# Linear attention with a gated feed-forward block: w2 loaded on the ScalarE queue, layer norms ahead of key finals, two tiny reads at the head

## The chip, the cores and the metric

One core of a Trainium2 chip runs the whole program. The metric is the device time of one execution in microseconds (us), median of several executions. A profile is one more execution, traced; its times are counted from the first instruction and its span is a little shorter than the device time (239.8 against 241.5 us for the profiled run of the kernel before). Engine names in the profile: PE is TensorE's matmuls, PEld its weight loads, DVE is VectorE, ACT is ScalarE, POOL is GpSimd, SP is SyncE; "SPq" and "ACTq" are the two that issue DMAs here.

## The reference, cut to what matters

The input x has 2048 tokens of 640 features, in bf16. The kernel normalizes it, and computes a linear attention and a relu feed-forward of the same normalized x:

```
xn  = layernorm(x)
q,k,v = split(xn @ wqkv)                  # 32 heads of 20
pq, pk = phi(q), phi(k)                   # phi(t) = (t+1 if t>0 else exp(t)) + 1e-6
kv  = sum over tokens of pk * v ;  z = sum over tokens of pk
s   = (pq @ kv) / (pq . z + 1e-6) @ wo
g   = silu(relu(xn @ w1) @ w2)            # w1: 640x1728, w2: 1728x640
out = x + s * g
```

## The kernel before

The program is written per engine: each operation is put on one engine's list in program order, with the waits that its reads and writes need. An engine takes its list strictly in order. So the order of the lines below is the order on each engine, and an operation that waits holds all that come behind it on the same engine (the load of w2 is held so until 134.8 us, as shown below).

The 2048 tokens are 16 tiles of 128, or four chunks j = 0 to 3 of 512. Chunk 0 is only centred at first (its scale is applied when its products are evicted), transposed on TensorE, and feeds the keys of tiles 0 to 3 and the w1 products `H_block(0, f)`. Tiles 4 to 15, and later tiles 0 to 3 for their queries, are normalized on VectorE and transposed by DMA. The helpers that matter:

```
def aggr(t):                    # VectorE: mean and variance; GpSimd: (var + eps) ** -0.5
    sc.op("DVE", bn_aggr -> mv[t]); sc.op("POOL", add -> rsv[t]); sc.op("POOL", pow -> rsy[t])
def LN_norm(t):                 # VectorE: (x - mean) * rsy, bf16 128x640; then x for tile t+8 is loaded
    last_norm[0] = sc.op("DVE", ... xn[:, t, :] ...)
    if t + XR < T: x_load(t + XR)
def xnT_dma(t):                 # SyncE queue: DMA transpose of xn[t] into xnT
def K_mm(t, b) / K_exp / K_relu # key product of a tile; two ScalarE evictions (exp, relu)
def K_fin(t):                   # VectorE: min(exp, 1) + 1e-6, then add relu -> pk[t]
    zpend.append(t)
def z_add():                    # GpSimd: zacc += pk[t]   (f32 128x640)
    t = zpend.pop(0)
    sc.op("POOL", ... tensor_tensor(out=zacc, in0=zacc, in1=pk[:, t, :], op=ALU.add))
def Q_block(j, f):              # five matmuls; ScalarE exp; two VectorE instructions -> pqT
```

The main loop walks the w1 blocks ("h") and query blocks ("q") of each chunk as TensorE's work, and hangs everything else on item numbers n:

```
kat  = [{5: 4, 7: 5, 9: 6, 11: 7}, {7: 8, 11: 9, 15: 10, 19: 11}, {6: 12, 9: 13, 12: 14, 15: 15}, {}]
lnat = [{0: 4, 2: 5, 4: 6, 6: 7}, {0: 8, 4: 9, 8: 10, 12: 11}, {0: 12, 3: 13, 6: 14, 9: 15}, {}]
for j in range(J):
    for n, item in enumerate(plans[j]):
        ... Q_block or H_block ...
        if n in lnat[j]:
            t = lnat[j][n]
            LN_stats(t)
            if j == 0:
                K_fin(t - 4)
                LN_norm(t);     xnT_dma(t)
                LN_norm(t - 4); xnT_dma(t - 4)
        ...                                   # j > 0: LN_norm and xnT_dma one item later
        if n in kat[j]: K_mm, K_exp, K_relu, K_fin of tile kat[j][n]
        if n >= 3 and zpend and len(zpend) > (1 if j < J - 1 else 0):
            z_add()
        ...                                   # chunk 3: z_split at n=2, z_col at 8, den() at 14
```

`den()` computes the denominator's reciprocal, writes it 20-fold to DRAM (`scr`, four writes of 640 KB) and reads it back (five reads). After the loop, on SyncE's queue, in this order: the `scr` writes and reads of `den()`, w2 (which waits for the last w1 product, as it takes w1's place), wo. Then TensorE computes `G_block(0..4)` (160 matmuls of keys against xn) and the w2 products `U_sub`, which fill the rest of the program.

## Time and profile before

Time before: 240.54 us median of 3 runs (240.16 to 243.49). From the first two parts of the page: the span is 239.8 us, and TensorE is busy for most of it.

```profile
...
PE 219.2 (91%) x1425; PEld 134.0 (56%) x1436; DVE 112.5 (47%) x211; ACT 87.8 (37%) x144; POOL 45.0 (19%) x69
...
PEclk9999999999999999999999995799999999999998
...
```

The first line is each engine's busy time, share of the span and number of instructions. The second cuts the span into 40 slices of 6 us: the clock granted to TensorE, in tenths. It drops to half in slices 24 and 25 (counted from 0); the trace has half clock from 142.8 to 153.0 us. As TensorE is 91% busy, what can be won is mostly its idle time. The list of waits of TensorE (engine, line, what it waited for; us in total, times, longest) says where that is:

```profile
PE psT L811 <- DMA reg<-in_B_w_dram: 9.5, 1, 9.5
PE psT L471 <- DMA reg<-reg: 2.9, 3, 2.3
PE psT L471 <- DMA reg<-in_A_wqkv_dram: 1.7, 1, 1.7
...
PE psT L471 <- ACT hT L550: 0.7, 1, 0.7
...
```

The first is the w2 product waiting for w2; the second is key products of tiles 4 to 15 waiting for a DMA transpose (2.3 us at 32.8 us is the longest); the third is the first key product waiting for its weights. The chain of waits (start, duration, what) shows why w2 is late:

```profile
...
114.74 3.36 DVE regE L660
...
121.77 10.71 DMA scr<-regE
...
134.30 0.47 SPq L672
...
135.31 13.15 DMA reg<-in_B_w_dram
...
148.55 3.62 PE psT L811 x13
...
```

The reciprocal (L660) ends at 118.1, the fourth write of `scr` lands at 132.5, the five reads behind it are issued until 134.8, only then is w2 issued, and it lands at 148.5. TensorE had finished G at 139.04. The clock was cut during that long idle stretch, 3.75 us after it began, and stayed so until 153.0: the first 13 w2 matmuls took 3.62 us, later sets in this chain mostly 1.77.

### The profile page before, as it was taken

The page shows a single profiled execution, that of the slowest core. Times are in us where ns is not written, and L with a number is a line of the kernel's source. Part 1 is how long each engine was busy: PE and PEld are TensorE (multiplying, and loading weights), DVE is VectorE, ACT ScalarE, POOL GpSimd, SP SyncE. Part 2 cuts the span into 40 slices and gives each one's busy share as a digit, 9 for nine tenths or more (in the row PEclk, how much of TensorE's full clock was granted, in tenths as well). Part 3 has the DMA queues.
Part 4 walks back from the last instruction along what each step waited for, and adds up shares of the span by engine and source line. Part 5 has one row for each costly group of instructions (what it writes and reads, how often), then busy time and mean ns, then how long its engine had stood idle before and what let it go on. Part 6 is the DMA issues. An engine that isn't in the chain of part 4 may idle for free.

```text
span 239.8 us, 3474 instructions
## 1 busy us (share of the span) xinstructions
PE 219.2 (91%) x1425; PEld 134.0 (56%) x1436; DVE 112.5 (47%) x211; ACT 87.8 (37%) x144; POOL 45.0 (19%) x69
## 2 busy tenths in 40 slices
PE   6899969999999989999999912999999999999994
PEld 5554434555545544444577701767776776777672
DVE  3388995999847981560600000482132432224143
ACT  5496635566655655554212130023202110210211
POOL 2154673333241365200000050000000000000000
PEclk9999999999999999999999995799999999999998
DMA  6998740511101120000099799920010101000011
GB/s 190 353 296 178 165 113 12 164 29 27 31 0 27 30 52 3 0 0 3 15 211 211 262 386 338 363 79 0 3 55 27 57 27 55 30 27 29 28 55 56
DMA packets 26992, 23.90 MB, mean 100 GB/s; under 512 B 11744, under 2 KB 26336, under 8 KB 26976
## 3 DMA queue, kind: packets, MB, share of 16 engines
q1 hardware_dynamic: 25664, 21.80, 31.2%
q10 hardware_dynamic: 1312, 1.88, 2.4%
q8 instruction: 11, 0.18, 0.3%
q14 instruction: 5, 0.04, 0.1%
HBM read 15.81 MB, written 5.24 MB: 88 GB/s over the span
## 4 chain that ended last, share of the span: by engine, by line
PE 64%; DMA 14%; DVE 13%; SPq 3%; POOL 2%; issue 2%; ACT 1%; DVEq 0%
PE psT L811 25%; PE psT L546 13%; PE psT L850 8%; PE psT L524 8%; PE psT L471 6%; DMA reg<-in_B_w_dram 5%; DMA scr<-regE 4%; DVE reg L413 3%; DVE stats L394 3%; DMA reg<-reg 2%; DMA reg<-in_A_wqkv_dram 2%; POOL rsy L402 2%; DVE pqT L534 2%; SPq L666 1%; DVE regE L660 1%
## 5 line engine op out<-in xcount | busy, mean ns | idle before, releaser
L811 PE MATMUL psT<-reg,hT 128*128 128x320 bf16 x416 | 62.2, 304 | 9.5 <-DMA reg<-in_B_w_dram 9.5
L811 PEld LDWEIGHTS psT<-reg,hT 128*128 128x128 bf16 x416 | 40.8, 99 | 27.1 <-issue 10.9
L546 PE MATMUL psT<-reg 128*128 128x512 bf16 x191 | 45.5, 379 | 0.3 <-issue 0.2
L550 ACT ACTIVATE hT<-psT 128x512 bf16<-128x512 f32 x52 | 30.9, 600 | 18.3 <-PE psT L546 18.3
L864 DVE TENSOR_TENSOR reg<-psT,reg 128x640 bf16<-128x640 f32 (+1 forms) x17 | 13.3, 785 | 48.8 <-PE psT L850 47.6
L546 PEld LDWEIGHTS psT<-reg 128*128 128x128 bf16 x195 | 19.0, 98 | 22.1 <-ACT hTl L567 0.4
L482 POOL TENSOR_TENSOR zacc<-zacc,reg 128x640 f32<-128x640 f32 x16 | 23.0, 1435 | 7.9 <-DVE reg L506 7.6
L850 PE MATMUL psT<-reg,pqT 128*128 128x320 bf16 x160 | 24.3, 299 | 0.0
L524 PE MATMUL psT<-reg 128*128 128x512 bf16 x95 | 23.8, 379 | 0.3
L839 ACT ACTIVATE reg<-psT 128x640 bf16<-128x640 f32 x12 | 8.2, 702 | 43.1 <-PE psT L811 23.6
L759 PE MATMUL psT<-reg 128*128 128x320 bf16 x160 | 21.9, 299 | 0.0
L471 PE MATMUL psT<-reg 128*128 128x320 bf16 x120 | 18.3, 299 | 3.6 <-DMA reg<-reg 2.9
L488 ACT ACTIVATE regE<-psT 128x640 bf16<-128x640 f32 x24 | 15.6, 701 | 13.4 <-PE psT L471 13.4
L759 PEld LDWEIGHTS psT<-reg 128*128 128x128 bf16 x160 | 15.7, 98 | 6.2
L850 PEld LDWEIGHTS psT<-reg,pqT 128*128 128x128 bf16 x160 | 15.7, 98 | 6.1
L532 DVE TENSOR_SCALAR regE<-psT 128x512 bf16<-128x512 f32 x20 | 13.6, 680 | 11.3 <-ACT regE L531 11.3
L413 DVE TENSOR_SCALAR reg<-reg,mv,rsy 128x640 bf16<-128x640 bf16 x16 | 16.5, 1051 | 3.3 <-POOL rsy L402 3.3
L777 DVE TENSOR_TENSOR reg<-psT,mv 128x120 bf16<-128x120 f32 (+1 forms) x6 | 1.5, 268 | 34.8 <-PE psT L774 34.8
L471 PEld LDWEIGHTS psT<-reg 128*128 128x128 bf16 x120 | 11.3, 97 | 11.2 <-ACT hT L550 3.0
L839 ACT ACTIVATE reg<-psT,rsy 128x640 bf16<-128x640 f32 x4 | 3.2, 794 | 35.3 <-PE psT L829 30.1
L524 PEld LDWEIGHTS psT<-reg 128*128 128x128 bf16 x100 | 9.7, 98 | 11.4
L534 DVE SCALAR_TENSOR_TENSOR pqT<-regE 128x512 bf16<-128x512 bf16 x20 | 15.3, 766 | 0.7
(68 smaller groups left out, 175.8 us busy)
## 6 DMA issues: line engine op xcount, KB each, us to landing
reg<-in_A_x_dram SPq DMA_DIRECT2D x16, 160.0 KB, 2.8
scr<-regE SPq DMA_DIRECT2D x4, 640.0 KB, 8.7
reg<-in_A_x_dram SPq DMA_DIRECT2D x4, 640.0 KB, 10.6
out_dram<-reg SPq DMA_DIRECT2D x15, 160.0 KB, 1.8
reg<-in_B_w_dram SPq DMA_DIRECT2D x2, 1120.0 KB, 9.1
regE<-scr SPq DMA_DIRECT2D x4, 512.0 KB, 5.2
reg<-in_B_w_dram ACTq DMA_DIRECT2D x1, 1040.0 KB, 5.2
reg<-in_B_w_dram SPq DMA_DIRECT2D x1, 960.0 KB, 13.2
```

Source lines behind the costliest of these rows:

```text
L413: last_norm[0] = sc.op("DVE", lambda eng: eng.tensor_scalar(out=xn[:, t, :], in0=xin[:, t % XR, :], scalar1=mv[:, t, 0:1], scalar2=rsy[:, ...
L471: fns.append(lambda eng, a=a, k=k, lhs=lhs: eng.matmul(ps[b + a][:, 0:HN], lhsT=lhs[:, k, tok(t)], rhs=wqk[:, k, D + HN * a:D + HN * (a + 1)],
L482: sc.op("POOL", lambda eng: eng.tensor_tensor(out=zacc[:, :], in0=zacc[:, :], in1=pk[:, t, :], op=ALU.add), R=[("zacc",), ("pk", t)], W=[( ...
L488: sc.op("ACT", lambda eng: eng.activation(out=o_.rearrange("p (a n) -> p a n", a=2), in_=ps2(b, HN), func=func, scale=scale), R=[("ps", b) ...
L524: sc.group("PE", [(lambda eng, k=k: eng.matmul(ps[b], lhsT=wqk[:, k, P * f:P * (f + 1)], rhs=xnT[:, k, schunk(j)], start=(k == 0), stop=(k ...
L532: sc.op("DVE", lambda eng: eng.tensor_scalar(out=r_, in0=ps[b], scalar1=0.0, scalar2=1e-6, op0=ALU.max, op1=ALU.add), R=[("ps", b), ("er_e ...
L534: sc.op("DVE", lambda eng: eng.scalar_tensor_tensor(out=pqT[:, f, schunk(j)], in0=e_, scalar=1.0, in1=r_, op0=ALU.min, op1=ALU.add), R=[(" ...
L546: a = sc.group("PE", [(lambda eng, k=k: eng.matmul(ps[b], lhsT=w1_sb[:, k, P * f:P * (f + 1)], rhs=src[:, k, :], start=(k == 0), stop=(k = ...
L550: sc.op("ACT", lambda eng: eng.activation(out=hT[:, f, schunk(j)], in_=ps[b], func=ACTF.Relu), R=[("ps", b)], W=[("hT", j, f)])
L759: fns.append(lambda eng, t=t, a=a: eng.matmul(ps[b + a][:, 0:HN], lhsT=xn[:, t, P * k:P * (k + 1)], rhs=pk[:, t, HN * a:HN * (a + 1)], sta ...
L811: sc.group("PE", [(lambda eng, f=f: eng.matmul(ps[b][:, 0:HN], lhsT=hT[:, f, tok(t)], rhs=w2_sb[:, f, HN * n:HN * (n + 1)], start=(f == 0 ...
L850: sc.group("PE", [(lambda eng, c=c, a=a: eng.matmul(ps[b + a][:, 0:HN], lhsT=pqT[:, c, tok(t)], rhs=wf[:, c, HN * a:HN * (a + 1)], start=( ...
```

## The change

The intent is to give w2 its own queue so that it no longer stands behind `scr`; to get tiles 4 to 7 normalized and transposed sooner in chunk 0 by doing their norms ahead of the key finals and of the norms of tiles 0 to 3, and by taking GpSimd's additions out of chunk 0; to start the denominator and the load of wo earlier; and to shorten the head (wk first, in smaller pieces, with two tiny reads meant to take the slow first packets of wqkv and w1). The core of the diff:

```
+    tch = nc.alloc_sbuf_tensor("tch", [16, 2, 64], bf)
+    for i, src in enumerate((A_wqkv, B_w1)):
+        dma("ACT", ... dma_start(tch[:, i, :], src[0:16, 0:64]) ...)
-    KA = 3
+    KA = 2
...                                # wk's two pieces move one place forward; 32 + 6 filler matmuls for 28
-    bn(1, 0)                      # in the head: first half of tile 1's statistics ...
+    bn(1, 0)                      # ... now behind ScalarE's evictions of tile 0 (with bn(1, 1), aggr(1))
...
-    lnat = [{0: 4, 2: 5, 4: 6, 6: 7}, {0: 8, 4: 9, 8: 10, 12: 11}, {0: 12, 3: 13, 6: 14, 9: 15}, {}]
+    lnat = [{0: 4, 1: 5, 2: 6, 3: 7}, {0: 8, 3: 9, 6: 10, 9: 11}, {0: 12, 2: 13, 4: 14, 6: 15}, {}]
+    zfrom = [99, 10, 8, 0]
...
                 if j == 0:
-                    K_fin(t - 4)
+                    if n >= 2:
+                        K_fin(2 * n - 4)
+                        K_fin(2 * n - 3)
                     LN_norm(t)
                     xnT_dma(t)
-                    LN_norm(t - 4)
-                    xnT_dma(t - 4)
+            if j == 0 and 4 <= n < 8:
+                LN_norm(n - 4)
+            if j == 0 and 8 <= n < 12:
+                xnT_dma(n - 8)
...
-            if n >= 3 and zpend and len(zpend) > (1 if j < J - 1 else 0):
+            if n >= zfrom[j] and zpend and j < J - 1:
                 z_add()
...                                # chunk 3: wo loaded at n=0; z_split, z_col, den at n = 1, 6, 11 for 2, 8, 14
-        dma("SP", ... w2_sb ...)   # both pieces of w2, and both copies of its last 64 rows
+        dma("ACT", ... w2_sb ...)
```

More of the change, by code (lines that the diff above doesn't have):

```diff
@@ L342, in w_load @@
         dma(E, lambda eng: eng.dma_start(dst, src.rearrange("(c p) n -> p c n", p=P)), W=[key], extra=extra)
-    KA = 3
+    tch = nc.alloc_sbuf_tensor("tch", [16, 2, 64], bf)
+    for i, src in enumerate((A_wqkv, B_w1)):
+        dma("ACT", lambda eng, i=i, src=src: eng.dma_start(tch[:, i, :], src[0:16, 0:64]), W=[("tch", i)])
+    KA = 2
     F1 = 7 * P
     x_load(0)
+    w_load(wqk[:, 0:KA, D:2 * D], A_wqkv[0:KA * P, D:2 * D], ("wk", 0))
     x_load(1)
-    w_load(wqk[:, 0:KA, D:2 * D], A_wqkv[0:KA * P, D:2 * D], ("wk", 0))
+    w_load(wqk[:, KA:C, D:2 * D], A_wqkv[KA * P:D, D:2 * D], ("wk", 1))
     x_load(2)
-    w_load(wqk[:, KA:C, D:2 * D], A_wqkv[KA * P:D, D:2 * D], ("wk", 1))
     x_load(3)
@@ L365, in bass_recurrent_scan__linear_attn_block__dense_activation_relu__prompt_kernel, with fill @@
     sc.op("POOL", lambda eng: eng.memset(zacc[:, :], 0.0), W=[("zacc",)])
-    NWARM = 28
-    sc.group("PE", [(lambda eng: eng.matmul(ps[7][:, 0:P], lhsT=zero[:], rhs=zero[:], start=True, stop=True))
-                    for _ in range(NWARM)], R=[("zero",)], W=[("ps", 7)])
+    def fill(n):
+        sc.group("PE", [(lambda eng: eng.matmul(ps[7][:, 0:P], lhsT=zero[:], rhs=zero[:], start=True, stop=True))
+                        for _ in range(n)], R=[("zero",)], W=[("ps", 7)])
     sc.allow_unread.add(("ps", 7))
+    fill(32)
     def build_consts():
@@ L576, in bass_recurrent_scan__linear_attn_block__dense_activation_relu__prompt_kernel @@
     centre(0)
-    mean_act(1, 0)
     transposes(0, 0)
@@ L580, in bass_recurrent_scan__linear_attn_block__dense_activation_relu__prompt_kernel @@
     xcT_copy(0, 0, 1)
-    centre(1)
-    K_mm(0, 2, 0, TS)
+    mean_act(1, 0)
+    fill(6)
     bn(0, 1)
     aggr(0)
-    mean_act(2, 0)
-    K_mm(0, 2, TS, KA)
+    centre(1)
+    K_mm(0, 2, 0, KA)
     transposes(1, 6)
@@ L589, in bass_recurrent_scan__linear_attn_block__dense_activation_relu__prompt_kernel @@
     xcT_copy(1, 6, 1)
+    K_mm(0, 2, KA, C)
+    mean_act(2, 0)
     centre(2)
-    K_mm(0, 2, KA, C)
-    mean_act(3, 0)
     K_mm(1, 4, 0, TS)
@@ L599, in bass_recurrent_scan__linear_attn_block__dense_activation_relu__prompt_kernel @@
     K_mm(1, 4, TS, C, (1,))
+    mean_act(3, 0)
+    centre(3)
     w_load(w1_sb[:, :, F1:FF], B_w1[:, F1:FF], ("w1", 1), E="ACT")
@@ L602, in bass_recurrent_scan__linear_attn_block__dense_activation_relu__prompt_kernel @@
     K_relu(0, 2)
-    centre(3)
+    bn(1, 0)
     bn(1, 1)
@@ L727, in bass_recurrent_scan__linear_attn_block__dense_activation_relu__prompt_kernel @@
                 build_consts()
+            if j == J - 1 and n == 0:
+                for c in range(VC):
+                    r0 = VR * c if c < VC - 1 else D - P
+                    dma("SP", lambda eng, c=c, r0=r0: eng.dma_start(wo_sb[:, c, :], A_wo[r0:r0 + P, :]),
+                        W=[("wo", c)], extra=[last_norm[0]])
             if j == J - 1:
@@ L730, in bass_recurrent_scan__linear_attn_block__dense_activation_relu__prompt_kernel @@
                     z_add()
-                if n == 2:
+                if n == 1:
                     z_split()
-                if n == 8:
+                if n == 6:
                     z_col()
-                if n == 14:
+                if n == 11:
                     lastW1 = H_half(0)
@@ L741, in bass_recurrent_scan__linear_attn_block__dense_activation_relu__prompt_kernel @@
         c0, c1 = (0, 7) if a == 0 else (7, NF)
-        dma("SP", lambda eng, c0=c0, c1=c1: eng.dma_start(
+        dma("ACT", lambda eng, c0=c0, c1=c1: eng.dma_start(
             w2_sb[:, c0:c1, :], B_w2[P * c0:P * c1, :].rearrange("(c p) n -> p c n", p=P)),
@@ L745, in bass_recurrent_scan__linear_attn_block__dense_activation_relu__prompt_kernel @@
     for u in range(2):
-        dma("SP", lambda eng, u=u: eng.dma_start(w2l[64 * u:64 * (u + 1), :], B_w2[NF * P:FF, :]),
+        dma("ACT", lambda eng, u=u: eng.dma_start(w2l[64 * u:64 * (u + 1), :], B_w2[NF * P:FF, :]),
             W=[("w2l", u)], extra=[lastW1])
-    for c in range(VC):
-        r0 = VR * c if c < VC - 1 else D - P
-        dma("SP", lambda eng, c=c, r0=r0: eng.dma_start(wo_sb[:, c, :], A_wo[r0:r0 + P, :]),
-            W=[("wo", c)], extra=[last_norm[0]])
     def G_block(k, b):
```

## The prediction

> **What bounds the kernel before.** TensorE: the page gives it 219.2 of 239.8 us busy. The list of waits and the timeline give its idle stretches: 9.51 us at 139.0 (for w2), 2.30 at 32.8 and 0.33 at 28.8 (for tiles transposed by DMA), 1.73 at 5.1 (for wk), 0.65 at 84.7, 0.29 at 90.1. The clock line shows half clock near 143-153 us, after the long gap: the first 13 matmuls of the w2 product took 3.62 us, later sets 1.77.
>
> **1. w2 on the ScalarE queue (the largest part).** In the chain of waits w2 stands behind the denominator: reciprocal until 118.1, four scr writes until 132.5, five reads of scr, then w2, issued at 134.8, landed at 148.5. TensorE ended the G product at 139.0. Afterwards w2 waits only for the last w1 matmul, so it is issued as the G product starts, which takes 21.9 us. It shares the DMA engines with the scr writes: those alone took 14.4 us at about 95% busy; w2 is 1792 packets of 55 ns over 16 engines, 6.2 us. The Trainium skill, "DMA: Bandwidth & Descriptors" (Queues, rings and completion order), has each engine take turns between queue rows by packets; in any order the sum is 20.6 us (estimate), counted from the scr start, now some 2 us before the G product (the denominator moves three blocks, 3.2 us, earlier). w2 lands 18-19 us into the G product, 3 us before need. The gap shrinks to the eviction of the last G block, about 0.8: gain 8.7. Without a long idle the clock is not lowered ("TensorE: Matmul & The Clock Gate", What's actually happening: an idle window of about 3.4 us halves it; this trace agrees): gain 1.85 on the first set, about 0.4 on the next: 2.2.
>
> **2. Norms ahead of key finals, running sum later.** Norms took 0.43-0.45 us when GpSimd was not adding, 1.51-1.55 when one of its 1.4 us zacc additions overlapped (instructions of that line). No addition now runs in chunk 0. Per tile: about 1.1 (stats) + 1.05 (GpSimd round trip, partly filled) + 0.44. The fourth norm ends near 26 instead of 33.3, tile 7's transpose lands near 29 instead of 34.9, and the 2.6 us of gaps go. The first chunk-1 query block needs tiles 0-3, landing about 35.7; TensorE reaches it at about 35.8 instead of 38.8: gain 3.0. The 0.65 and 0.29 gaps of chunk 2: I count 0.7.
>
> **3. Head.** wk's first piece is smaller and earlier: landing 6.7 becomes about 5; the tiny reads may absorb the slow first packets (up to 1.0 us in the trace), or only move them onto x. But the first w1 block (15.2) is released by ScalarE's evictions, whose chain is hardly shorter. I count 0.3.
>
> **Sum:** 8.7 + 2.2 + 3.0 + 0.7 + 0.3 = 14.9 us of 240.5. Off the critical path: wo, xre, divisions.
>
> **Predicted: 225.8 us, 80% range 223.0 to 230.0.** Faster by over 2%: 0.97; within 2%: 0.025; slower: 0.005.
>
> **What would show it.** TensorE idle under 1.2 us between G and the first w2 matmul, released by ScalarE; full clock there, first 13 matmuls about 1.8 us; all chunk-0 norms about 0.44 us; no DMA-transpose wait over 1 us before 40 us; G begins near 113.
>
> **What would make it wrong.** w2 starved by the scr writes; ScalarE blocked in its DMA issues so that G evictions stall TensorE (slack about 4 us); scr reads so late that the divisions hold VectorE's evictions of the W blocks; a head slowed by the tiny reads.

## The result, and the profile after

The changed kernel took 231.2 us median (230.69 to 233.07, 4 runs) against 241.1 (240.16 to 243.49, 4 runs) of the kernel before: ratio 0.9585, 95% interval 0.9508 to 0.9662. A ratio here is the mean time of one kernel's runs over that of the other's runs of the same rounds, so it is not quite the ratio of the medians quoted. Executions over 1.5% slower than the fastest of the same kernel are left out of the means. The kernel got faster by about 10 us where 14.9 were predicted, and 231.2 lies outside the predicted range of 223.0 to 230.0. The same two lines of the page, for the changed kernel:

```profile
...
PE 218.0 (94%) x1436; PEld 133.8 (58%) x1446; DVE 109.0 (47%) x211; ACT 87.8 (38%) x144; POOL 46.8 (20%) x69
...
PEclk9999999999999799999999999999999999999999
...
```

The clock no longer drops near 143 us, but there is a new dip in slice 13 (counted from 0): half clock from 76.9 to 80.3 us. TensorE's list of waits (same columns as before):

```profile
PE psT L477 <- DMA reg<-reg: 3.1, 1, 3.1
...
PE psT L552 <- ACT regE L494: 0.9, 1, 0.9
PE psT L822 <- ACT reg L775: 0.8, 1, 0.8
PE psT L530 <- DMA reg<-reg: 0.7, 1, 0.7
PE psT L552 <- DVE regE L538: 0.6, 1, 0.6
...
```

The wait for w2 is gone: the first w2 product (L822) waits 0.8 us for the eviction of the last G block, as predicted, and its first 13 matmuls took 1.94 us (predicted: about 1.8). But the wait of a key product for a DMA transpose, which the change was to remove, is as large as before, 3.1 us in one piece. The timeline below places it at 74 us, in chunk 2, before the key product of tile 12. The kernel before had no wait there (one would stand in brackets at the end of the line):

```profile
75.32 1.52 PE L471 MATMUL psT<-reg 128*128 128x320 bf16 x10
```

Its own long wait was at 32.8 us, in chunk 0. Its two short waits in chunk 2, of 0.65 and 0.29 us, which the prediction counted as gain, are gone in the changed kernel. A table of moments in the profiles shows where the time went (us from the start of the span, from the timelines):

| moment | before | changed | gained in this stretch |
|---|---|---|---|
| first query block (it needs the transposes of tiles 0 to 3) | 38.81 | 36.70 | 2.1 |
| key product of tile 12 (chunk 2) | 75.32 | 77.18 | -4.0 |
| G begins | 117.15 | 119.26 | -0.2 |
| first w2 product | 148.55 | 141.95 | 8.7 |
| end | 239.80 | 231.33 | 1.9 |

The two lower rows are the w2 part: 8.7 us of gap and 1.9 us of clock and after, predicted 8.7 and 2.2. All of what the change gained in chunk 0, and more, was lost between 37 and 77 us. The -0.2 of the row "G begins" hides a second loss: the run e5 below, at full clock, takes 40.56 us from tile 12 to G, this one 42.08, so the half clock after the gap cost about 1.5 us. G begins at 119.26, where about 113 was predicted. (The profiled execution is the slowest of the changed kernel's, 233.07 us. Its granted clock is 0.991; the others have 0.997 to 0.999 and did not go through a long half-clock stretch.)

This is the timeline of the changed kernel before the gap (start, duration, engine, line, operation, output<-inputs, count, idle time before it and what ended it):

```profile
...
48.73 0.49 DVE L512 TENSOR_TENSOR reg<-regE 128x640 bf16<-128x640 bf16 x1
...
52.53 18.07 POOL L488 TENSOR_TENSOR zacc<-zacc,reg 128x640 f32<-128x640 f32 x11
...
55.88 1.52 DVE L510 TENSOR_SCALAR regE<-regE 128x640 bf16<-128x640 bf16 x1
...
57.43 1.60 DVE L512 TENSOR_TENSOR reg<-regE 128x640 bf16<-128x640 bf16 x1
...
68.17 1.17 DVE L540 SCALAR_TENSOR_TENSOR pqT<-regE 128x512 bf16<-128x512 bf16 x1
...
69.27 1.52 DVE L510 TENSOR_SCALAR regE<-regE 128x640 bf16<-128x640 bf16 x1
...
71.23 0.88 DVE L400 BATCH_NORM_STATS2 stats<-reg 128x6 f32<-128x320 bf16 x2
...
72.14 0.21 DVE L404 BATCH_NORM_AGGREGATE mv<-stats 128x2 f32<-128x12 f32 x1
...
72.82 0.23 POOL L406 TENSOR_SCALAR rsv<-mv 128x1 f32<-128x1 f32 x1
...
74.09 0.45 DVE L419 TENSOR_SCALAR reg<-reg,mv,rsy 128x640 bf16<-128x640 bf16 x1 [0.46 <-POOL rsy L408]
...
77.18 2.85 PE L477 MATMUL psT<-reg 128*128 128x320 bf16 x10 [3.06 <-DMA reg<-reg]
...
```

Eleven additions to `zacc` run back to back on GpSimd from 52.5 to 70.6 us, a twelfth from 71.5. In that time the two instructions of a key final (L510 and L512) take 1.52 and 1.60 us; with no addition beside them they take 0.32 and 0.49 in the same profile (the pair that ends at 49.2 us, for one). The second instruction of a query block (L540) takes 1.17 instead of 0.69. VectorE falls behind; it reaches the statistics of tile 12 (L400) at 71.2 us, its norm at 74.1, and the transpose that TensorE waits for lands at 77.1. The statistics were complete at 72.35 and GpSimd took them up (L406) at 72.82: only these 0.47 us are a queue on GpSimd.

Adding up, over VectorE's instructions between the first query block and tile 12's key product, what each took above its undisturbed time (norm 0.443, L510 0.322, L512 0.493, L540 0.692 us; excesses under 0.1 us left out) gives 9.3 us in the changed kernel and 3.7 in the kernel before.

The w2 part, in the timeline of the changed kernel, with the queues' issues:

```profile
...
117.00 5.65 SPq L672 DMA_DIRECT2D scr<-regE  x4
...
119.47 2.21 ACTq L758 DMA_DIRECT2D reg<-in_B_w_dram  x2
121.71 5.30 ACTq L762 DMA_DIRECT2D reg<-in_B_w_dram  x2
127.06 0.70 ACT L775 ACTIVATE reg<-psT 128x640 bf16<-128x640 f32 x1 [7.00 <-issue]
...
```

w2 is issued as G starts, beside the `scr` writes. The last of both landed at 136.3 us, 19.3 us after the first `scr` issue, where I had estimated 20.6. (The 95% in that estimate holds for the stretch from 120 to 131 us; over all of the 14.4 us the DMA engines were 80% busy.) The landings of the two queues interleave: w2's two large pieces landed at 131.6 and 135.9 us, the third and fourth `scr` writes at 131.9 and 135.9. That agrees with the Trainium skill, "DMA: Bandwidth & Descriptors" (Queues, rings and completion order), by which each DMA engine takes packets from the rings in turn: from 128 to 134 us the trace has 1027 packets of the one queue and 1024 of the other. ScalarE was held in its four DMA issues for 7.5 us, until 127.0, so the first G eviction (L775) came 3.4 us after G's first block was done. It cost TensorE nothing in this profile, but it used up nearly all of the slack of about 4 us that the prediction named: in the runs e4 and e6 below, where the issues ended 8.1 and 8.4 us after the first began, G waited 0.2 and 0.5 us for it.

### The profile page after: what moved, and what is told of

It is laid out like the page before. It is cut to its first block, busy times and chain, and to the rows that moved or that the text cites. A ratio compares the mean times of both kernels' runs of the same rounds, so it can differ in the third digit from the quotient of the medians.

```text
span 231.3 us, 3500 instructions
## 1 busy us (share of the span) xinstructions
PE 218.0 (94%) x1436; PEld 133.8 (58%) x1446; DVE 109.0 (47%) x211; ACT 87.8 (38%) x144; POOL 46.8 (20%) x69
## 4 chain that ended last, share of the span: by engine, by line
PE 71%; DVE 13%; DMA 5%; issue 3%; SPq 3%; ACT 2%; POOL 2%; DVEq 0%; POOLq 0%
PE psT L822 25%; PE psT L552 14%; PE psT L770 9%; PE psT L861 9%; PE psT L477 5%; PE psT L530 4%; DVE regE L538 2%; DMA reg<-in_A_wqkv_dram 2%; DMA reg<-reg 2%; DVE pqT L540 2%; DVE regE L510 2%; DVE reg L512 2%; SPq L468 2%; DVE stats L400 1%; DVE reg L419 1%
## 5 line engine op out<-in xcount | busy, mean ns | idle before, releaser
L822 PE MATMUL psT<-reg,hT 128*128 128x320 bf16 x416 | 60.5, 299 | 0.8 <-ACT reg L775 0.8
L822 PEld LDWEIGHTS psT<-reg,hT 128*128 128x128 bf16 x416 | 40.2, 98 | 17.5 <-ACT reg L775 1.1
L556 ACT ACTIVATE hT<-psT 128x512 bf16<-128x512 f32 x52 | 30.9, 601 | 19.3 <-PE psT L552 19.3
L552 PEld LDWEIGHTS psT<-reg 128*128 128x128 bf16 x195 | 18.9, 98 | 22.9 <-DVE regE L538 1.1
L488 POOL TENSOR_TENSOR zacc<-zacc,reg 128x640 f32<-128x640 f32 x16 | 24.3, 1518 | 10.6 <-DVE reg L512 9.8
L530 PE MATMUL psT<-reg 128*128 128x512 bf16 x95 | 24.0, 382 | 1.0 <-DMA reg<-reg 0.7
L477 PE MATMUL psT<-reg 128*128 128x320 bf16 x120 | 19.6, 313 | 3.1 <-DMA reg<-reg 3.1
L770 PE MATMUL psT<-reg 128*128 128x320 bf16 x160 | 21.9, 299 | 0.0
L770 PEld LDWEIGHTS psT<-reg 128*128 128x128 bf16 x160 | 15.7, 98 | 6.2
L477 PEld LDWEIGHTS psT<-reg 128*128 128x128 bf16 x120 | 12.1, 102 | 10.4 <-DMA reg<-reg 3.6
L540 DVE SCALAR_TENSOR_TENSOR pqT<-regE 128x512 bf16<-128x512 bf16 x20 | 17.3, 865 | 0.7
L530 PEld LDWEIGHTS psT<-reg 128*128 128x128 bf16 x100 | 9.8, 99 | 12.5 <-DMA reg<-reg 1.0
L537 ACT ACTIVATE regE<-psT 128x512 bf16<-128x512 f32 x20 | 11.9, 597 | 9.8 <-PE psT L530 9.8
L552 PE MATMUL psT<-regX,reg 128*128 128x512 bf16 x63 | 14.4, 379 | 0.9 <-ACT regE L494 0.9
L400 DVE BATCH_NORM_STATS2 stats<-reg 128x6 f32<-128x320 bf16 x32 | 14.1, 480 | 2.1 <-DMA reg<-in_A_x_dram 2.1
```

Source lines behind the costliest of these rows:

```text
L400: sc.op("DVE", lambda eng: eng.bn_stats(stats[:, t, a, :], xv[:, HN * a:HN * (a + 1)]), R=[("xin", t % XR)], W=[("stats", t, a)])
L477: fns.append(lambda eng, a=a, k=k, lhs=lhs: eng.matmul(ps[b + a][:, 0:HN], lhsT=lhs[:, k, tok(t)], rhs=wqk[:, k, D + HN * a:D + HN * (a + 1)],
L488: sc.op("POOL", lambda eng: eng.tensor_tensor(out=zacc[:, :], in0=zacc[:, :], in1=pk[:, t, :], op=ALU.add), R=[("zacc",), ("pk", t)], W=[( ...
L530: sc.group("PE", [(lambda eng, k=k: eng.matmul(ps[b], lhsT=wqk[:, k, P * f:P * (f + 1)], rhs=xnT[:, k, schunk(j)], start=(k == 0), stop=(k ...
L540: sc.op("DVE", lambda eng: eng.scalar_tensor_tensor(out=pqT[:, f, schunk(j)], in0=e_, scalar=1.0, in1=r_, op0=ALU.min, op1=ALU.add), R=[(" ...
L552: a = sc.group("PE", [(lambda eng, k=k: eng.matmul(ps[b], lhsT=w1_sb[:, k, P * f:P * (f + 1)], rhs=src[:, k, :], start=(k == 0), stop=(k = ...
```

## The experiments

Theory A: GpSimd's additions, deferred out of chunk 0, are packed into chunk 1, and each slows the VectorE instructions that overlap it; VectorE, nearly full in that chunk, falls behind, and tile 12's norm is late. The Trainium skill, "SBUF — State Buffer" (Who interferes with whom), names the mechanism: VectorE and GpSimd share one pair of SBUF ports under an exclusive lock; by that section a VectorE instruction in a two-port mode contends with any GpSimd instruction, and one with two SBUF inputs only with a GpSimd instruction that reads SBUF, not with one that only writes. Rival B: it is only the queue: GpSimd computes tile 12's scale, and twelve additions of 1.4 us stand ahead of it. Rival C: the new head or the new order of norms does it, without the additions.

The runs were timed against the kernel before, which is the denominator of every ratio below. Its runs spread from 239.2 to 245.5 us. Runs e1 to e4 were on one chip, e5 to e8 on a second and e9 to e11 on a third, each with its own runs of the kernel before, so ratios compare better across them than times.

### The additions replaced by writes of the same length

```
-        sc.op("POOL", ... tensor_tensor(out=zacc, in0=zacc, in1=pk[:, t, :], op=ALU.add),
-              R=[("zacc",), ("pk", t)], W=[("zacc",)])
+        junk = [("hT", 3, f) for f in (10, 11, 12)]       # not yet in use
+        sc.op("POOL", ... memset(hT[:, 10:13, 1536:2048], 0.0), R=[("zacc",), ("pk", t)], W=[("zacc",)] + junk)
```

> The changed kernel, but each GpSimd addition to zacc is replaced by a GpSimd memset of about the same length (1536 elements, about 1.4 us) at the same place and with the same waits; the result is wrong on purpose. In the changed kernel TensorE idles 3.06 us at 74 us, before the key product of tile 12. Theory A (the twelve additions packed into chunk 1 slow the VectorE instructions that overlap them, VectorE falls behind): memsets read nothing, so VectorE's key finals in chunk 1 return from 1.52 to about 0.33 us and from 1.60 to 0.49 us, the gap falls under 0.7 us, time about 227.5 to 228.5 us. Rival B (the statistics of tile 12 only queue behind twelve GpSimd instructions of 1.4 us): GpSimd is as full as before, gap stays 2.5 to 3.5 us, time about 231. Rival C (the new head or the new order of norms makes it): gap stays, about 231.

The result is wrong. 227.7 us median, ratio 0.9466. The memsets took 1.38 to 1.50 us each in chunk 1, at the same places in the queue. The gap before tile 12's key product was 0.56 us instead of 3.06. The timeline of this run (columns as above):

```profile
...
51.38 7.30 POOL L490 MEMSET hT<- 128x1536 bf16 x5
...
53.57 0.69 DVE L542 SCALAR_TENSOR_TENSOR pqT<-regE 128x512 bf16<-128x512 bf16 x1
...
54.53 0.49 DVE L514 TENSOR_TENSOR reg<-regE 128x640 bf16<-128x640 bf16 x1
...
57.59 1.27 DVE L512 TENSOR_SCALAR regE<-regE 128x640 bf16<-128x640 bf16 x1
...
64.59 0.21 DVE L404 BATCH_NORM_AGGREGATE mv<-stats 128x2 f32<-128x12 f32 x1
...
68.83 0.22 POOL L406 TENSOR_SCALAR rsv<-mv 128x1 f32<-128x1 f32 x1
...
```

With GpSimd about as full as before but reading nothing, no two-input instruction of VectorE was slowed at all (all 16 of L514 took 0.49, all 20 of L542 0.69 us; this run's lines are numbered two higher than above), while a one-input instruction in a fast mode still was at times (L512 1.27). That is the distinction that the skill's section makes, and this run agrees with it. VectorE's excess in the stretch falls to 2.6 us. Theory A stands; B and C, which expected a gap of 2.5 us and more, fall as the cause of the 3.06 us. But B is real, and it explains the 0.56 us that are left. Here VectorE had tile 12's statistics ready at 64.8 us (72.35 in the changed kernel), and GpSimd took them up only at 68.83, after the last memset: 4.0 us of queue, 2.7 of which VectorE sat idle. In the changed kernel VectorE was so late that the same queue cost 0.47 us.

### The old rule for the additions, and additions at the end of chunk 0

```
-            if n >= zfrom[j] and zpend and j < J - 1:
+            if n >= 3 and zpend and len(zpend) > (1 if j < J - 1 else 0):      # e2
-    zfrom = [99, 10, 8, 0]
+    zfrom = [8, 10, 8, 0]                                                      # e4
```

> The changed kernel with the placing of the zacc additions put back to the old rule (from the fourth item on, one kept pending); new order of norms kept. That puts 7 additions into chunk 0 behind the last statistics, 4 into chunk 1. Theory A: gap before tile 12's key product under 1 us, time 227.5 to 229; some of chunk 0's last norms or key finals 1.5 us, which costs at most about 1 us. Rival B: the same sign (fewer instructions ahead of tile 12's statistics). Rival C: gap of about 3 us stays, time about 231.

> The changed kernel with additions allowed from item 8 of chunk 0 (where VectorE idles 2 us at a time), which takes five of the twelve out of chunk 1. Theory A: each addition in chunk 1 delays VectorE by about 0.5 to 1.2 us, so five fewer take 2.5 to 5 us of delay away: gap under 0.7 us, time 227.5 to 228.5. Rival B: the queue ahead of tile 12 is also shorter, gap falls likewise; only the memset run tells A from B. Rival C: gap stays about 3 us, 231.

Both missed: 233.87 us (ratio 0.9729) and 233.69 us (0.9716), no faster than the changed kernel (medians 231.2 and, on another chip, 232.86; the intervals of the ratios overlap). In both the gap in chunk 2 was gone, which theory A expected, but a larger one had opened at the end of chunk 0. From the timeline of the second of them, e4 (columns as above):

```profile
...
24.59 6.05 POOL L488 TENSOR_TENSOR zacc<-zacc,reg 128x640 f32<-128x640 f32 x4
...
24.87 4.47 DVE L419 TENSOR_SCALAR reg<-reg,mv,rsy 128x640 bf16<-128x640 bf16 x3
...
28.05 5.45 SPq L339 DMA_DIRECT2D reg<-in_A_x_dram  x4
...
```

TensorE's list of waits of the same run:

```profile
PE psT L530 <- DMA reg<-reg: 4.8, 1, 4.8
...
```

I had put the additions at item 8 and thought of item 8's time on TensorE. But GpSimd does not wait for TensorE's items: its first four additions need only the key finals of tiles 0 to 3, which VectorE had done between 21.3 and 25.0 us, so it began them at 24.6 us, when its scales were finished. That was right under the norms of tiles 7, 0 and 1, which took 4.47 us for three where the changed kernel has 1.16. The reloads of x and the four transposes behind them were late, and the first query block (L530) waited 4.8 us. From 3.3 and 3.4 us into this wait the clock was halved for 6.8 us in the two profiles. So the same additions do the same harm in chunk 0, where another chain is short of slack.

### Additions at the end of chunk 0, held until the norms are done

```
+    def z_add(extra=()):                       # passed on to sc.op(..., extra=extra)
-    zfrom = [99, 10, 8, 0]
+    zfrom = [8, 10, 8, 0]
-                z_add()
+                z_add([last_norm[0]] if j == 0 else ())
```

> As the run e4_adds_chunk0_tail, but the additions of chunk 0 also wait for chunk 0's last norm. In e4 the GpSimd queue took four of them at 24.6 us, right under the norms of tiles 0 to 3 (4.47 us for three instead of 1.16), and TensorE then idled 4.8 us for their transposes. Theory A: now five additions run from about 27.7 to 35 us, under key finals that have slack, and seven instead of twelve stay in chunk 1: norms of tiles 0 to 3 back at 0.44 us, TensorE waits about 0.7 us at 36 as in the changed kernel, gap before tile 12's key product under 0.8 us, time 227.5 to 228.7. If A is wrong about dose (seven back to back harm as much as twelve): gap about 3, time 231.

226.89 us (226.49 to 227.64), ratio 0.9429 against the changed kernel's 0.9585: about 4 us, from an edit of a few lines with no work added or taken away. It is a little more than expected (227.5 to 228.7). Five additions now run from 27.4 to 34.9 us, all eight norms of chunk 0 take 0.44 or 0.45 us, and neither wait for a transpose is left in TensorE's list of waits. The additions in this run's timeline, and then that list:

```profile
...
27.36 7.57 POOL L488 TENSOR_TENSOR zacc<-zacc,reg 128x640 f32<-128x640 f32 x5 [2.96 <-DVE reg L419]
...
```

```profile
...
PE psT L552 <- ACT regE L494: 0.9, 1, 0.9
PE psT L822 <- ACT reg L775: 0.8, 1, 0.8
PE psT L452 <- DVE reg L443: 0.6, 2, 0.4
PE psT L477 <- ACT regX L464: 0.5, 1, 0.5
...
```

VectorE's excess in the stretch is 5.4 us, against 9.3 in the changed kernel and 3.7 before: 5.4 still fits into VectorE's slack there, 9.3 does not.

### Each part of the change alone

The w2 loads alone on the ScalarE queue, and the new order of norms with the deferred additions alone, each applied to the kernel before:

```
-        dma("SP", ... w2_sb ...); dma("SP", ... w2l ...)                        # e3
+        dma("ACT", ... w2_sb ...); dma("ACT", ... w2l ...)
```

> The kernel before with only the four w2 loads moved to the ScalarE queue (wo, denominator, norms, head as before). If w2's place is the whole gain of the change: 229.5 to 231 us. My sum for this part was 8.7 for the gap and 2.2 for the clock, so 229.6; the scr writes start here only 1 us after the G product starts instead of 2 us before it, so w2 may land just at need: gap between G and the first w2 product 0.8 to 2.5 us, full clock there. [...]

230.61 us (229.14 to 231.32), ratio 0.9581: this part alone gives what the whole change gives. In its trace the wait before the first w2 product is 0.8 us, and the clock stays up; the span shrinks from 239.80 to 228.82, that is 10.98 us, of which 0.4 are luck: the head, which this run does not touch, ran 0.4 us faster. w2, issued here just ahead of the `scr` writes, had landed by 128.1 us, and its issues held ScalarE for only 2.4 us. It needed neither the earlier denominator nor the earlier wo.

> The kernel before with only the new order of norms and the deferred additions (w2, wo, denominator, head as before). My prediction counted 3.0 + 0.7 = 3.7 us for this part: 237. Theory A now: about 2 us gained in chunk 0 and about 3 us lost before tile 12's key product in chunk 2 (a gap of 2.5 to 3.5 us in the trace, sometimes followed by half clock); net 0 to +1.5 us: 240 to 242.5, no gain against the kernel before. The long wait for w2 remains.

242.53 us (241.96 to 242.6), ratio 1.006, interval 0.9998 to 1.0123: no gain. It is this part that the prediction had counted at 3.7 us. Its trace has the first query block at 36.57 us, 2.2 earlier than before, and a gap of 3.10 us before tile 12's key product, after which the clock stayed full.

### The head

```
-    for i, src in enumerate((A_wqkv, B_w1)):
-        dma("ACT", ... dma_start(tch[:, i, :], src[0:16, 0:64]) ...)            # e6
-    bn(1, 0); bn(1, 1); aggr(1)      # behind K_relu(0), moved ahead of centre(3)  # e7
```

> The changed kernel without the two tiny reads. My reading: the first w1 block is released by ScalarE's eviction behind the scale of tile 1 (GpSimd, 13.67 us), and Q(0,0) by the transposes of tiles 0 to 3; neither hangs on the first loads. So first w1 block within 0.4 us of 15.5 and time within 0.8 us of the changed kernel's 231.1. If the reads do what they are meant to: wk's first piece lands over 0.8 us later than 4.65, first w1 block later by as much, time 231.5 to 232.5.

232.03 us (231.44 to 232.54), ratio 0.9639. Without the tiny reads wk's first piece landed at 4.57 us, with them at 4.65 and 4.43 in the two profiles of the changed kernel, and in the kernel before at 6.71. So the earlier landing comes from the smaller piece and its place in the queue, and the reads show no effect on it. The time was expected within 0.8 us of 231.1 and is 0.9 above it; the spread of the changed kernel itself (230.69 to 233.73 in its timed runs) is larger, so an effect of the reads on the time is not shown.

> The changed kernel with the statistics of tile 1 put ahead of the centring of tile 3. In the changed kernel ScalarE's eviction of key tile 1 waited until 13.71 us for that tile's scale. Expected: eviction near 13.0, first w1 block near 14.8 instead of 15.5 us; but the transposes of tiles 0 to 3 still land near 36.4, so the wait before the first query block grows from 0.74 to about 1.4 us and the time moves by less than 0.4 us from the changed kernel's. If the head were the limit of chunk 0: 0.7 us faster.

232.1 us (229.9 to 232.39), ratio 0.9622. ScalarE's eviction no longer waits: TensorE's idle time before the first w1 block shrank from 0.88 to 0.06 us. The total did not move beyond the spread. I had expected the gain to come back as a longer wait of the first query block, 1.4 us; that wait was 0.41 us and the block began at 35.79, within the two profiles of the changed kernel (36.70 and 35.73). So where the gain went is not shown. The head itself varies by as much: the first w1 block began between 14.69 and 15.47 us in seven profiles with the new head that lack this edit (one of them without the tiny reads), and between 14.79 and 15.60 in three with the old one.

### All repairs together, and the changed kernel once more

> Four repairs of the changed kernel at once: additions as in e5_adds_after_norms, statistics of tile 1 early as in e7_rsy1_early, the reloads of x for tiles 8 to 11 issued after the transposes of tiles 0 to 3 instead of before them (2 us of the SyncE queue), and the last G block in banks 4 and 5 so that the first w2 product need not wait for its eviction. Sum if each holds: 3.0 (gap in chunk 2) + 0.7 (wait for the query block) + 0.7 (head, now no longer hidden) + 0.8 (between G and w2) = 5.2 us: 226.0; range 225.3 to 228.

226.1 us (225.8 to 226.44), ratio 0.9389. The waits for the query block and the head are gone, but moving the last G block to other banks gained nothing: TensorE now ran on into the kv products and waited there 0.99 us: the eviction on VectorE waited for the memset of its target on GpSimd, which the longer wait had hidden.

```
-    sc.op("POOL", ... memset(kvp, 0.0), W=[("kvz",)], extra=[lastG])
+    for c in range(VC):
+        sc.op("POOL", ... memset(kvp[:, c, :], 0.0), W=[("kvz", c)], extra=[lastG])
```

> e8_combined plus one edit: the 3.3 us GpSimd memset of the kv blocks, which TensorE waits for (0.99 us inside the kv products in e8, once G and the w2 product adjoin), is cut into six memsets of about 0.6 us, one per block. Expected: that wait falls under 0.3 us; 226.1 - 0.8 = 225.3 us, range 224.6 to 226.3. If the time does not move, the wait has only gone elsewhere.

> The changed kernel itself, unedited, beside e9_best and e10_norms_alone on one chip, to compare them directly and to see how often the gap of 3 us in chunk 2 is followed by half clock. Expected 230.5 to 232.5 us, gap of 2.9 to 3.2 us before tile 12's key product in the profile.

On one chip: 224.87 us (224.52 to 224.88, ratio 0.9329) for the repaired kernel and 232.86 us (230.91 to 233.73, ratio 0.9641) for the changed one; the repaired one, which is correct, beats both kernels. TensorE's whole list of waits in it:

```profile
PE psT L452 <- DVE reg L443: 1.1, 2, 0.8
PE psT L371 <- DVE zero L361: 1.1, 1, 1.1
PE psT L477 <- ACT regX L464: 0.5, 1, 0.5
PE psT L477 <- DMA reg<-in_A_wqkv_dram: 0.2, 1, 0.2
PE psT L552 <- issue: 0.2, 1, 0.2
```

The four runs of the changed kernel also show why its times spread. Its gap of 3.06 us is sometimes followed by half clock and sometimes not: the run with a granted clock of 0.999 took 230.91 us, the one with 0.990 took 232.28, the two with 0.985 took 233.44 and 233.73. In the profile of the 233.44 us run the clock was halved for 6.8 us, from 2.2 us into the gap on. The repaired kernel, with no such gap, has a clock of 1.00 in all four runs and a spread of 0.36 us.

## Why the prediction was wrong

- **Step 1, w2: right, in mechanism and size.** Predicted 8.7 us of gap and 2.2 us of clock. The stretch from G to the first w2 product shrank by 8.7 us and the rest by 1.9 us, and the run with this part alone gained all of it. The remaining wait of 0.8 us for ScalarE was as foreseen.
- **Step 2, chunk 0: right.** "No addition now runs in chunk 0": all its norms took 0.44 to 0.45 us. The first query block came 2.1 and 3.1 us earlier in the two profiles of the changed kernel (36.70 and 35.73 against 38.81); predicted 3.0.
- **Step 2, chunk 2: wrong; this is the step that failed.** "The 0.65 and 0.29 gaps of chunk 2: I count 0.7" as gain. Those two gaps did go, but a new one of 3.06 us opened ahead of them: 3.97 us were lost between the first query block and tile 12's key product (40.48 us against 36.51), and in some runs half clock on top (about 1.5 us in the profile). I had read from the trace of before that an addition makes an overlapped norm take 1.5 us instead of 0.44, noted that the additions leave chunk 0, and never asked where they go: twelve of them into chunk 1, nearly back to back, beside VectorE, which was busy 23.5 of the 25.9 us from the first query block on (the view by stretches, kernel before, 38.8 to 64.7 us). I treated the deferral as free.
- **Step 3, head: off the critical path, as I half expected.** I counted 0.3; the first w1 block moved from 15.25 to 15.47 and 15.16, and in the run with the head's wait removed the time did not move beyond the spread.
- **The sum.** The run that only puts the additions elsewhere has the first query block 3.2 us earlier than before (35.59), the same time from there to tile 12 (36.52 against 36.51), 1.3 us less until G, 8.7 less until w2 and 1.9 less after: 15.05 us of span, where I had predicted 14.9; G begins at 112.67. So the other terms were about rightly sized. That the sum fits so closely is partly luck: these are single profiles, of a run 0.5 us above the mean of the kernel before and one 0.5 us below that of e5. By the mean of the runs e5 gains 14.0 us and the changed kernel 10.0, on different chips: this one term is about 4 of the 4.9 us that were missing, and the rest stays open.

## What to carry to other kernels

Work that is deferred out of a critical stretch lands somewhere: before you defer it, look at what runs beside it in its new place, and count the slowdown of the engine that shares memory ports with it as a cost there (here 9.3 us of VectorE's time against 3.7). Moving an operation by program order alone does not fix when it runs: in e4 GpSimd, with a free queue, started it as soon as its inputs were ready, at 24.6 us, so hold it with an explicit dependency on the work that it must not disturb. After the longest wait is removed, test each remaining part alone: here one part gave the whole gain, and the rest summed to about nothing until the additions were moved and held by one dependency.

## What the Trainium skill lacked or had wrong

- "TensorE: Matmul & The Clock Gate" (What's actually happening) gives at least one idle window of about 3.4 us for the drop to half clock, and says that the window runs freely, so that the moment of a change varies. Here a shorter stretch was enough: in two profiles of the changed kernel half clock began 2.2 and 2.8 us into the gap of 3.06 us (by the profile's modelled matmul ends; 0.4 us more from the last matmul's start), and lasted 6.8 and 3.4 us. In the run e10 a gap of 3.10 us was followed by none. One program so took 230.91 to 233.73 us. Gaps of 4.8 us brought 6.8 us of half clock in both profiles that had one, gaps of 9.5 and 9.8 us 10.24.
- "DMA: Bandwidth & Descriptors" (Issuing engines are not separate DMA queues) says that a second issuing engine only saves issue time, which is usually small. That says nothing of the order within one engine's queue: here the second queue gained 8.7 us of TensorE's idle time, because w2 no longer stood behind writes and reads that wait for each other. On the pages I read I found no figure for how long an issue can hold its engine when much is outstanding: four issues held ScalarE 7.5 us, where a free issue took about 0.4.
- "SBUF — State Buffer" (Who interferes with whom) agrees with the runs in which VectorE's times were compared here. It says that the instruction that comes second is blocked until the first is done; the sizes for these shapes are not there: one GpSimd addition of 1.4 us turns VectorE instructions of 0.44, 0.32, 0.49 and 0.69 us into 1.51, 1.52, 1.60 and 1.17, and is itself stretched to as much as 1.73.
